# First-norm rows stored four tiles at a time behind phase one, with w2 and the first w3 loads behind the tile transposes

## The chip, the cores and the metric

One NeuronCore of a Trainium2 chip. The metric is device time in microseconds of one execution of the whole kernel, the median of several runs. The engines are named as in the profile: TensorE (PE, with its weight loads as PEld), VectorE (DVE), ScalarE (ACT), GpSimd (POOL) and SyncE (SP), which here only issues DMAs. Sixteen DMA engines move the data for all of them.

## What is computed

The input x has 2048 rows of 1024. It is normalised row by row, xn = norm(x), and the result is a sum of three terms:

```python
xn = layernorm(x)
out = x + A(xn, mem0, Wq, Wk, Wv, Wo, seg_len) + B(xn, w1, w2, w3, w4)
# B: a shifted MLP
h  = gelu(layernorm(xn) @ w1)                 # 1024 -> 1024
hs = shift_quarters(h) @ w2                   # four column groups moved by -1, +1, -2, +2 rows
x1 = xn + hs
B  = x1 + gelu(layernorm(x1) @ w3) @ w4       # 1024 -> 3584 -> 1024
# A: 64 segments of 32 rows; attention of 32 heads over 8 memory rows + 32 rows,
#    the first 8 output rows of a segment are the memory of the next
```

All inputs are bf16. The change touches B's beginning only; A begins after B and reads xn back from a scratch tensor in DRAM.

## The kernel before, in words

Rows are handled in 16 tiles of 128. There are four parts that matter here.

**Phase one** (lines 219 to 405) makes h transposed, `hTB`, in SBUF. For tile n, `load_x(n)` brings the rows in (a ring of ten buffers). `norm_stats(n)` takes the row statistics on VectorE and two powers on POOL (L272): one for the first norm, one for the norm of the norm, which is a different scale of the same row. From tile 8 on POOL also makes a bias `nm2` (L274). `norm2(n)` writes the twice-normed row tile `xn2` (VectorE for n < 8, L281; ScalarE from 8 on, L283). The tile is then transposed: by TensorE for the first six (`tr`, L305), by a DMA transpose on SP's queue from tile 6 on (L285), into `xn2T`, a ring of three pairs of tiles. `stage1` (L321) multiplies one or two tiles by w1, eight column blocks with eight matmuls each, and ScalarE evicts each block with the gelu (L328) through four PSUM buffers. `norm1(n)` writes the once-normed rows into SBUF, `xn_keep` (L291), four tiles to a buffer, and stores them in DRAM as `xn_scratch` (L292, POOL's queue).

**Phase two** (lines 407 to 433) takes 16 tiles through w2 (L417, two halves of eight matmuls), adds `xn_keep` on VectorE (L418), norms with POOL's and ScalarE's help, transposes the result by a DMA on SP's queue (L430) into `xn3T`, and stores x1 in DRAM from POOL's queue (L431).

**Phase three** (lines 435 to 581) is w3, gelu and w4, in four blocks of four tiles (L546 and L572). During its first block the sums of xn over segments are made from `xn_scratch` (L450), and in its last block `xn_scratch` is read again, transposed, for part A (L567). `xn_keep` lives until the end of phase two.

**Part A** follows: L603 (values), L669 (queries and keys), L684 to L727.

The order of work on TensorE, VectorE, ScalarE, POOL and SP is the order in which the program is written; `between` and `prep` say behind which column block of which stage the norms of later tiles are put. A DMA waits on its issuing queue until the transfer that used its semaphore before is finished. There are eight of these semaphores for the hardware queues, used in turn, so at most eight such transfers are open.

w2 is loaded in four pieces of 512 KB on SP's queue ahead of x7 (L250). w3 comes in eight pieces of 896 KB (`load_w3`): two within phase one, two within phase two, four behind it.

Of the kernel before, what the change touches and what calls it, by code (L numbers as in the profile page):

```python
# [27 lines left out]
NT = S // P  # L28
# [49 lines left out]
def kernel(  # L78
# [16 lines left out]
    nc = tc.nc  # L95
# [7 lines left out]
    w2_v = B_w2.rearrange("(k p) n -> p k n", p=P)  # L103
    w3_v = B_w3.rearrange("(k p) n -> p k n", p=P)
# [7 lines left out]
    xn_v = xn_d.rearrange("(n p) d -> p n d", p=P)  # L112
# [78 lines left out]
    with tc.manual_schedule(engines={mybir.EngineType.PE, mybir.EngineType.SP, mybir.EngineType.Pool}), ExitStack() as actx:  # L191
# [6 lines left out]
        with ExitStack() as bctx:  # L198
            w3ctx = bctx.enter_context(ExitStack())
            w3_pool = w3ctx.enter_context(tc.tile_pool(name="w3", bufs=1, side="right"))  # L200
            w3_sb = w3_pool.tile([P, KT, F], BF16)

            w3_at = [0]

            def load_w3():

                c, k0 = divmod(w3_at[0], 4)
                w3_at[0] += 1
                cs = slice(c * (F // 2), (c + 1) * (F // 2))
                nc.sync.dma_start(w3_sb[:, 2 * k0:2 * k0 + 2, cs], w3_v[:, 2 * k0:2 * k0 + 2, cs])  # L210

            with ExitStack() as hctx:
                psum0 = hctx.enter_context(tc.tile_pool(name="psum0", bufs=4, space=PSUM))
# [2 lines left out]
                w2_sb = keep.tile([P, KT, D], BF16)  # L216
                xn_keep = [wpool.tile([P, 4, D], BF16, tag="w", name=f"xnk{i}") for i in range(3)] + [keep.tile([P, 4, D], BF16, name="xnk3")]

                hctx.enter_context(tc.manual_schedule(engines={mybir.EngineType.DVE, mybir.EngineType.Activation}))
                with ExitStack() as p0:  # L220
# [7 lines left out]
                    def load_x(n):  # L228
                        if n < NT:
                            xts[n] = ring.tile([P, D], BF16, tag="xt", bufs=10, name=f"xt{n}")  # L230
                            if n == 0:
                                nc.scalar.dma_start(xts[n][:, 512:], x_v[:, n, 512:])
                                nc.sync.dma_start(xts[n][:, :512], x_v[:, n, :512])
                            else:
                                (nc.gpsimd if n == 12 else nc.sync).dma_start(xts[n][:], x_v[:, n, :])
# [10 lines left out]
                        q.dma_start(w1_sb[:, 2 * c:2 * c + 2, :], w1_v[:, 2 * c:2 * c + 2, :])  # L246
                    for n in range(3, 7):
                        load_x(n)
                    for i in range(4):
                        nc.sync.dma_start(w2_sb[:, 2 * i:2 * i + 2, :], w2_v[:, 2 * i:2 * i + 2, :])  # L250
                    for n in range(7, 10):
                        load_x(n)

                    stats = {}

# [32 lines left out]
                    def norm1(n):  # L288
                        st, mv, ab, rr, nm2 = stats[n]
                        xn = xn_keep[n // 4][:, n % 4]  # L290
                        nc.vector.tensor_scalar(xn, xts[n][:], mv[:, 0:1], rr[:, 0:1], op0=ALU.subtract, op1=ALU.mult)  # L291
                        nc.gpsimd.dma_start(xn_v[:, n, :], xn)  # L292
                        if n < 3:
                            load_x(n + 10)
                        if n in (12, 15):
                            load_w3()
                        return xn

                    def transposes(xn2, xn2T, jj, half, halves=False):
# [21 lines left out]
                    def stage1(n0, nt, xn2T, between, j0=0):  # L321
                        w = nt * P
                        for co in range(KT):
                            ps = psum.tile([P, 512], F32, tag="mm", bufs=4)
                            for k in range(KT):
                                nc.tensor.matmul(ps[:, :w].rearrange("p (n t) -> p n t", t=P), w1_sb[:, k, co * P:(co + 1) * P],  # L326
                                                 xn2T[:, j0:j0 + nt, k, :], start=(k == 0), stop=(k == KT - 1))
                            nc.scalar.activation(hTB[:, co, 2 + n0 * P:2 + n0 * P + w], ps[:, :w], ACTF.Gelu_apprx_tanh)  # L328
                            for f in between.get(co, ()):
                                f()  # L330
# [20 lines left out]
                    def tr(n, half, halves=False):  # L351
                        transposes(xn2s[n], tiles2[n - n % 2], n % 2, half, halves)
# [15 lines left out]
                    for n in range(1, 6):  # L368
                        if n > 1:
                            norm_stats(n + 1, 0)  # L370
                        norm2_of(n)
                        norm_stats(n + 1, 1 if n > 1 else None)
                        if n > 1:
                            norm1(n - 2)
                        if n == 1:
                            stage1_k(tiles2[0])
                        elif n < 4:
                            stage1(n - 1, 1, tiles2[(n - 1) // 2 * 2], {6 - n: [lambda n=n: tr(n, 0)], 7 - n: [lambda n=n: tr(n, 1)]}, (n - 1) % 2)

                    def ahead(n):  # L380
                        norm_stats(n + 1, 0)
                        norm2_of(n)
                        norm_stats(n + 1, 1)
                        if n == 6:
                            norm1(n - 2)

                    stage1(3, 1, tiles2[2], {0: [lambda: tr(4, 0)], 2: [lambda: tr(4, 1), lambda: ahead(6)], 4: [lambda: tr(5, 0)], 5: [lambda: tr(5, 1), lambda: ahead(7)]}, 1)
                    for n in range(13, NT):
                        load_x(n)

                    def prep(n):
                        norm2_of(n)
                        norm_stats(n + 1)
                        if n == 8:
                            norm1(n - 3)
                        norm1(n - 2)

                    for n0 in range(4, NT, 2):
                        between = {c: [] for c in range(KT)}
                        if n0 + 4 < NT:  # L400
                            between[1 + 2 * (n0 == 4)] += [lambda n0=n0: prep(n0 + 4)]
                            between[4 + 2 * (n0 == 4)] += [lambda n0=n0: prep(n0 + 5)]
                        stage1(n0, 2, tiles2[n0], between)
                    for n in (NT - 2, NT - 1):
                        norm1(n)

                xn3T = [wpool.tile([P, 4, KT, P], BF16, tag="w", name=f"xn3T{tb}") for tb in range(4)]
                with ExitStack() as p2:
                    ring = p2.enter_context(tc.tile_pool(name="p2ring", bufs=4))
                    for n in range(NT):  # L410
                        x1 = ring.tile([P, D], F32, tag="x1")
                        st = ring.tile([P, 2, 6], F32, tag="st")
                        for ch in range(2):
                            ps = psum.tile([P, 512], F32, tag="mm", bufs=4)
                            for k in range(KT):
                                o = 2 + n * P + SH[k]
                                nc.tensor.matmul(ps[:], hTB[:, k, o:o + P], w2_sb[:, k, ch * 512:(ch + 1) * 512], start=(k == 0), stop=(k == KT - 1))  # L417
                            nc.vector.tensor_tensor(x1[:, ch * 512:(ch + 1) * 512], ps[:], xn_keep[n // 4][:, n % 4, ch * 512:(ch + 1) * 512], op=ALU.add)  # L418
                            nc.vector.bn_stats(st[:, ch, :], x1[:, ch * 512:(ch + 1) * 512])
                        mv = ring.tile([P, 2], F32, tag="mv")  # L420
                        nc.vector.bn_aggr(mv[:], st[:])
                        a = ring.tile([P, 1], F32, tag="a")
                        nc.vector.tensor_scalar(a[:], mv[:, 1:2], EPS, None, op0=ALU.add)
                        r3 = ring.tile([P, 1], F32, tag="r3")
                        nc.gpsimd.tensor_tensor(r3[:], a[:], neghalf[:, 0:1], op=ALU.pow)
                        nm3 = ring.tile([P, 1], F32, tag="nm3")
                        nc.gpsimd.tensor_scalar(nm3[:], mv[:, 0:1], r3[:], -1.0, op0=ALU.mult, op1=ALU.mult)
                        xn3 = ring.tile([P, D], BF16, tag="xn3")
                        nc.scalar.activation(xn3[:], x1[:], ACTF.Identity, bias=nm3[:], scale=r3[:])
                        nc.sync.dma_start_transpose(xn3T[n // 4][:, n % 4], xn3[:])  # L430
                        nc.gpsimd.dma_start(R1_v[:, n, :], x1[:])  # L431
                        if n in (3, 7):
                            load_w3()

            with ExitStack() as p3:
# [2 lines left out]
                big = p3.enter_context(tc.tile_pool(name="p3big", bufs=1))  # L438
                ring = p3.enter_context(tc.tile_pool(name="p3ring", bufs=2))
                w4_sb = big.tile([P, FT, D], BF16)  # L440
                for _ in range(4):
                    load_w3()
                vbT = big.tile([P, H, NSEG], BF16)
                xb = big.tile([P, KT, NSEG], BF16)
                gps = []
# [95 lines left out]
                for tb in range(4):  # L541
# [18 lines left out]
                    for j in range(4):  # L560
                        n = tb * 4 + j
# [344 lines left out]
    with tc.If(cond > 0):  # L906
        with ExitStack() as fctx:
# [15 lines left out]
            with tc.For_i(0, NSEG, 1) as i:  # L923
# [6 lines left out]
                for which, src in enumerate((Wq_v, Wk_v, Wv_v)):  # L930
                    w = fw.tile([P, KT, H * DH], BF16, tag="w")
# [98 lines left out]
```

## Time and profile before

| | us |
|---|---|
| median of 4 runs | 1508.92 (1508.79 to 1509.85) |
| the profiled execution | 1508.89 |
| its span in the profile | 1506.7 |
| matmul time on TensorE in it | 1501.4 |
| phase one, first matmul to the first of phase two | 1.5 to 67.6 |
| phase two | 67.6 to 122.9 |
| phase three's first block, w3 then w4 | 122.9 to 219.6 (from 171.2 on w4) |

The DMAs issued in and around phase one, from the trace: SP issues the four w2 loads from 8.54 us on, x7 to x11 from 11.56 to 18.21, the transposes of tiles 6 and 7 at 24.49 and 27.16, x13 to x15 from 28.51 to 30.75, the transposes of tiles 8 and 9 at 31.34 and 33.29, the first two w3 loads at 51.27 and 53.88 and the last transpose of the phase, of tile 15, at 52.60. POOL issues the sixteen stores of 256 KB from 15.66 to 47.12 us; they land 4.6 us after they are issued in the median. The granted TensorE clock is 1.00 throughout.

How to read the lines shown below: the page's first part gives the busy time of each engine and its share of the span. A chain of waits is followed back from the last instruction: each line has its start, its length and what ran. A line of the waits names who waited for whom, the total, how often, and the longest. In a table by stretches the busy times come in the order PE, PEld, DVE, ACT, POOL, each with its number of instructions, then the clock, the share of time that the sixteen DMA engines were busy (overlapping packets can take it over 1) and what they moved in GB/s. "T6" and so on is used for the DMA transpose of tile 6 in phase one.

### The profile page before, as it was taken

To read this page: it belongs to the slowest core of one execution; us is meant where nothing else is said; L and a number is where in the kernel's file an instruction comes from. 1 tells how busy PE (TensorE), PEld (TensorE's weight loads), DVE (VectorE), ACT (ScalarE), POOL (GpSimd) and SP (SyncE) were. 2 spreads that over 40 slices of the span, in tenths; PEclk is the share of its full clock that TensorE was granted. 3 is DMA by queue.
4 is the path that set the end of the run, shared out by engine and by line. 5 is a ranking of instruction groups with operands and counts; after the bars stand their busy time and mean duration, and the time that the engine had idled before them with its cause. 6 is when DMAs were issued, how large, how long until landed. Compare 5 with 4: busy or idle time off the path is not lost.

```text
span 1506.7 us, 24319 instructions
## 1 busy us (share of the span) xinstructions
PE 1501.4 (100%) x9828; PEld 803.5 (53%) x9828; DVE 546.6 (36%) x1148; ACT 502.1 (33%) x1140; POOL 175.5 (12%) x250
## 2 busy tenths in 40 slices
PE   9999999999999999999999999999999999999999
PEld 8744444445454444444456645664665455545555
DVE  8382230100010112212246624651564166516643
ACT  5533203013012011111156614660663166406630
POOL 6231020211211221100000000001000100010001
PEclk9999999999999999999999999999999999999999
DMA  9699752453455777622389956992997298928921
GB/s 305 154 265 325 220 172 95 137 203 111 155 154 145 186 236 254 218 98 84 126 219 254 243 130 172 257 233 77 242 247 204 73 230 222 215 66 207 208 50 51
DMA packets 305426, 272.89 MB, mean 181 GB/s; under 512 B 156022, under 2 KB 272536, under 8 KB 305312
## 3 DMA queue, kind: packets, MB, share of 16 engines
q1 hardware_dynamic: 282656, 188.98, 50.0%
q0 software_dynamic: 21824, 81.08, 15.8%
q8 instruction: 79, 1.29, 0.4%
q10 hardware_dynamic: 832, 1.25, 0.2%
q14 instruction: 35, 0.29, 0.1%
HBM read 190.05 MB, written 45.29 MB: 156 GB/s over the span
## 4 chain that ended last, share of the span: by engine, by line
PE 99%; DMA 1%; ACT 0%; DVE 0%; issue 0%; ACTq 0%
PE ps L669 30%; PE pso L727 15%; PE ps L603 15%; PE ps L572 13%; PE ps L546 13%; PE ps L417 4%; PE ps L326 3%; PE psS L684 2%; PE psO L708 2%; DMA xn2T<-xn 1%; PE ps L498 1%; PE ps L867 1%; PE ps L467 0%; PE gps L481 0%; PE warm L343 0%; PE ps L316 0%
## 5 line engine op out<-in xcount | busy, mean ns | idle before, releaser
L669 PE MATMUL ps<-hTb,wt 128*128 128x396 bf16 (+2 forms) x2528 | 484.8, 342 | 0.0
L669 PEld LDWEIGHTS <-wt 128*128 128x128 bf16 x2528 | 236.8, 98 | 175.4 <-DMA wt<-in_A_Wq_dram 0.2
L603 PE MATMUL ps<-wt,xT 128*128 128x512 bf16 x1024 | 221.2, 379 | 0.0
L727 PE MATMUL pso<-wo_sb,oX 128*128 128x512 bf16 (+1 forms) x992 | 209.9, 372 | 0.0
L546 PE MATMUL ps<-xn3T,w_sb 128*128 128x512 bf16 x896 | 196.2, 379 | 0.0
L572 PE MATMUL ps<-w_sb,h3T 128*128 128x512 bf16 x896 | 195.4, 379 | 0.0
L603 PEld LDWEIGHTS <-xT 128*128 128x128 bf16 x1024 | 100.2, 98 | 120.8
L547 ACT ACTIVATE h3T<-ps 128x512 bf16<-128x512 f32 x112 | 67.0, 598 | 290.6 <-PE ps L546 289.7
L727 PEld LDWEIGHTS <-oX 128*128 128x128 bf16 x992 | 96.4, 98 | 107.6
L671 ACT CAST KT<-ps 128x462 bf16<-128x462 f32 (+2 forms) x160 | 81.8, 511 | 202.6 <-PE ps L669 198.4
L572 PEld LDWEIGHTS <-h3T 128*128 128x128 bf16 x896 | 87.1, 98 | 103.5
L546 PEld LDWEIGHTS <-w_sb 128*128 128x128 bf16 x896 | 86.7, 98 | 102.2
L690 DVE TENSOR_REDUCE sums<-sm 99x4 f32<-99x396 f32 (+2 forms) x176 | 97.6, 554 | 114.8 <-ACT sm L688 114.8
L673 ACT ACTIVATE QT<-ps 128x462 bf16<-128x462 f32 (+2 forms) x160 | 84.0, 525 | 120.5 <-PE ps L669 106.2
L605 ACT CAST Vs<-ps 128x512 bf16<-128x512 f32 x64 | 37.5, 586 | 232.1 <-PE ps L603 232.1
L686 DVE TENSOR_TENSOR sm<-psS,c_mask_reg_sb 99x396 f32<-99x396 f32 x152 | 86.7, 570 | 72.3 <-PE psS L684 72.2
L609 DVE CAST Vs<-ps 128x512 bf16<-128x512 f32 x64 | 44.3, 692 | 171.6 <-PE ps L603 171.6
L688 ACT ACTIVATE sm<-sm 99x396 f32<-99x396 f32 (+2 forms) x176 | 92.8, 527 | 34.7 <-DVE sm L686 28.1
L696 DVE TENSOR_TENSOR Pn<-sm,rs 99x396 bf16<-99x396 f32 (+2 forms) x176 | 98.9, 562 | 6.6 <-DMA PT<-Pn 0.7
L734 POOL DMA_DIRECT2D out_dram<-ot x30 | 16.4, 546 | 698.5 <-DVE ot L733 698.5
L573 DVE TENSOR_TENSOR R<-ps,R 128x512 f32<-128x512 f32 x32 | 22.0, 690 | 181.9 <-PE ps L572 173.0
L733 DVE TENSOR_TENSOR ot<-pso,Rt 128x512 bf16<-128x512 f32 (+1 forms) x33 | 22.2, 675 | 166.5 <-PE pso L727 162.3
(131 smaller groups left out, 1049.6 us busy)
## 6 DMA issues: line engine op xcount, KB each, us to landing
wt<-in_A_Wq_dram SPq DMA_DIRECT2D x76, 512.0 KB
wt<-in_A_Wk_dram SPq DMA_DIRECT2D x76, 512.0 KB
wt<-in_A_Wv_dram POOLq DMA_DIRECT2D x24, 1024.0 KB, 6.4
V_scratch<-Vs SPq DMA_DIRECT2D x32, 512.0 KB
V<-V_scratch SPq DMA_DIRECT2D x40, 384.0 KB
R_scratch<-x POOLq DMA_DIRECT2D x16, 512.0 KB, 4.3
R<-R_scratch SPq DMA_DIRECT2D x16, 512.0 KB
R_scratch<-R POOLq DMA_DIRECT2D x16, 512.0 KB, 3.4
```

Of the source, the lines that this page charges most:

```text
L546: nc.tensor.matmul(ps[:].rearrange("p (n t) -> p n t", t=P), w3_sb[:, k, f * P:(f + 1) * P], xn3T[tb][:, :, k, :], start=(k == 0), stop=(k ...
L547: nc.scalar.activation(h3T[:, f, :], ps[:], ACTF.Gelu_apprx_tanh)
L572: nc.tensor.matmul(ps[:], h3T[:, f, j * P:(j + 1) * P], w4_sb[:, f, ch * 512:(ch + 1) * 512], start=(f == 0), stop=(f == FT - 1))
L603: nc.tensor.matmul(ps[:], xT[:, m4 * 4 + j, k, :], wv[:, k, :], start=(k == 0), stop=(k == KT - 1))
L669: nc.tensor.matmul(ps[:, :nb], w[:, k, hh * P:(hh + 1) * P], B["hT"][:, k, :nb], start=(k == 0), stop=(k == KT - 1))
L671: nc.scalar.copy(dst[:, hh, :], ps[:, :nb])
L673: nc.scalar.mul(dst[:, hh, :], ps[:, :nb], scale)
L686: nc.vector.tensor_tensor(sm[:T, :, :T], S3, t["mask"][:].unsqueeze(1).to_broadcast((T, 4, T)), op=ALU.add)
L688: nc.scalar.activation(e[:T, :, :T], sm[:T, :, :T], ACTF.Exp, scale=LN2)
L690: nc.vector.tensor_reduce(ss, e[:T, :, :T], axis=AX.X, op=ALU.add)
L696: nc.vector.tensor_tensor(Pn[:T, :, :T], e[:T, :, :T], rs[:T, :].unsqueeze(2).to_broadcast((T, 4, T)), op=ALU.mult)
L727: nc.tensor.matmul(self.ps[:, :self.w], self.oX[0][:, h, self.oX[1] + self.gl * P:self.oX[1] + (self.gl + 1) * P], wo_sb[:, h, self.cc], s ...
```

## The change

The stores of the once-normed rows leave `norm1`. Behind the last `norm1` there are four stores of four tiles (1 MB) each, on SP's queue. w2 is loaded in two pieces of 1 MB, issued behind `stage1` of tiles 6 and 7 and of tiles 10 and 11, and so on SP behind the transposes of tiles 11 and 15. x13 to x15 are issued behind `stage1` of tiles 4 and 5, which puts them behind the transposes of tiles 8 and 9, where they were ahead of them. The first two w3 loads are issued behind the four stores, and the last four are two of double size.

The order of instructions on TensorE, VectorE and ScalarE stays as it was. On POOL sixteen DMA issues are gone. On SP there are two rows fewer and the order is the new one.

```diff
-            def load_w3():
+            def load_w3(w=1):
 
                 c, k0 = divmod(w3_at[0], 4)
-                w3_at[0] += 1
+                w3_at[0] += w
                 cs = slice(c * (F // 2), (c + 1) * (F // 2))
-                nc.sync.dma_start(w3_sb[:, 2 * k0:2 * k0 + 2, cs], w3_v[:, 2 * k0:2 * k0 + 2, cs])
+                nc.sync.dma_start(w3_sb[:, 2 * k0:2 * (k0 + w), cs], w3_v[:, 2 * k0:2 * (k0 + w), cs])
...
-                    for i in range(4):
-                        nc.sync.dma_start(w2_sb[:, 2 * i:2 * i + 2, :], w2_v[:, 2 * i:2 * i + 2, :])
                     for n in range(7, 10):
                         load_x(n)
+
+                    def load_w2(i):
+                        nc.sync.dma_start(w2_sb[:, 4 * i:4 * i + 4, :], w2_v[:, 4 * i:4 * i + 4, :])
...
                         nc.vector.tensor_scalar(xn, xts[n][:], mv[:, 0:1], rr[:, 0:1], op0=ALU.subtract, op1=ALU.mult)
-                        nc.gpsimd.dma_start(xn_v[:, n, :], xn)
                         if n < 3:
                             load_x(n + 10)
-                        if n in (12, 15):
-                            load_w3()
                         return xn
...
                     stage1(3, 1, tiles2[2], {0: [lambda: tr(4, 0)], 2: [lambda: tr(4, 1), lambda: ahead(6)], 4: [lambda: tr(5, 0)], 5: [lambda: tr(5, 1), lambda: ahead(7)]}, 1)
-                    for n in range(13, NT):
-                        load_x(n)
-
                     def prep(n):
...
                         stage1(n0, 2, tiles2[n0], between)
+                        if n0 == 4:
+                            for n in range(13, NT):
+                                load_x(n)
+                        elif n0 in (6, 10):
+                            load_w2(n0 // 10)
                     for n in (NT - 2, NT - 1):
                         norm1(n)
+                    for i in range(4):
+                        nc.sync.dma_start(xn_v[:, 4 * i:4 * i + 4, :], xn_keep[i][:])
+                    for i in range(2):
+                        load_w3()
...
-                for _ in range(4):
-                    load_w3()
+                for _ in range(2):
+                    load_w3(2)
```

## The prediction

> **What bounds the kernel now.** I read the page first, then the chain of waits and TensorE's waits over phase one, then busy time by stretches, then the queue of SP. The page says that TensorE is the bound:
>
> ```profile
> span 1506.7 us, 24319 instructions
> PE 1501.4 (100%) x9828; PEld 803.5 (53%) x9828; DVE 546.6 (36%) x1148; ACT 502.1 (33%) x1140; POOL 175.5 (12%) x250
> PE 99%; DMA 1%; ACT 0%; DVE 0%; issue 0%; ACTq 0%
> ```
>
> The reader is to see that only 1506.7 - 1501.4 = 5.3 us are left in which the matmul engine does not work, and that the one other entry on the chain, DMA 1%, is the tile transpose xn2T<-xn of phase one. So I look at that. The chain of waits from 20 to 70 us, in order of time (start, us, what):
>
> ```profile
> 24.49 5.48 DMA xn2T<-xn
> 29.97 0.02 issue
> ...
> 30.08 0.69 ACT xn L283
> ...
> 32.14 1.12 ACT xn L283
> 33.26 0.03 ACT hTB L328
> 33.29 6.09 DMA xn2T<-xn
> 39.38 0.14 issue
> 39.52 28.11 PE ps L326 x256
> ```
>
> Call the transpose of tile n Tn. T6, issued at 24.49, lands at 29.97; ScalarE's norm of tile 8 (L283) has waited for it; T9, issued at 33.29, lands at 39.38; TensorE's stage of tiles 8 and 9 starts at 39.52. From there to the end the chain is TensorE alone. TensorE's waits in that window have one entry (us, times, longest):
>
> ```profile
> PE ps L326 <- DMA xn2T<-xn: 0.7, 1, 0.7
> ```
>
> That is not all. From 39.52 on a stage of two tiles takes 64 matmuls; ScalarE's evictions behind every 8 of them come 0.873 us apart when nothing is late (46.70, 47.57, 48.45 in the timeline), so 6.99 us a stage. The first eviction of the stage of tiles 4 and 5 at 25.51 puts that stage's start at about 24.46. Two stages should end at 24.46 + 13.98 = 38.44, and the third starts at 39.52: **1.08 us are lost**, 0.73 in the wait shown and 0.35 at the border near 31.5 us, where ScalarE, held from 28.5 to 30.08 by T6, evicts three PSUM tiles late (31.22).
>
> The rest of phase one has no hole to fill: 11.93 to 24.43 us is 224 matmuls of 128 columns at 55.8 ns = 12.5 us, and the four stages after 39.52 and all of phase two run at an unchanging rate (55.25 us for 256 matmuls, 215.8 ns). The stretches show the room on the DMA side (engines' busy times, then clock, DMA share, GB/s):
>
> ```profile
> 25.00:30.00 5.00, 5.00 (x48) 4.49 (x46) 4.79 (x14) 1.54 (x4) 2.54 (x4) 1.00 1.19 197
> 35.00:40.00 5.00, 4.27 (x40) 3.62 (x39) 4.86 (x13) 3.20 (x8) 4.31 (x7) 1.00 1.20 246
> 60.00:65.00 5.00, 5.00 (x48) 4.48 (x47) 0.00 (x0) 2.11 (x6) 0.00 (x0) 1.00 0.01 5
> ```
>
> The DMA engines are full while T6 to T9 fly and idle from 60 to 75 us.
>
> **The change part by part**, against the profiled execution's own 1508.89 us (span 1506.7 and 2.2 around it; the median is 1508.92, so the two are the same).
>
> *Two w2 loads of 1 MB instead of four of 512 KB ahead of x7.* By 25 us the engines have moved 8.45 MB (the rates of five stretches times 5 us: 196, 386, 376, 381, 352 GB/s), and w2 is 2.1 of it. Without w2 the loads are done some 5.5 us sooner (2.1 MB at 380), so T6 finds empty queues. The x rows come earlier, which gains nothing: VectorE takes them in its own order and is busy 4.79 to 4.92 us of each 5 from 15 to 45 us.
>
> *Sixteen stores of 256 KB leave POOL's queue.* POOL loses 16 issues (10.1 us in all, 0.61 each). It is not on the chain, worth 0. But two of these stores are issued while T6 and T7 fly and five while T8 and T9 do.
>
> *What T6 to T9 then take.* T6 and T9 took 5.48 and 6.09 us. The nearest row with less beside it is the last transpose of phase two: issued 127.20, landed 130.88, so 3.68 us, still beside one 512 KB store. Bounds: 3.7 and 6.1; I take 4. T6 is issued when VectorE has made tile 6 (24.43), which does not move: it lands at 28.5. ScalarE's norm of tile 8 then waits for POOL's nm (29.20 + 0.27 = 29.47) and starts at 29.55 instead of 30.08; T8 at 30.85, tile 9's norm behind its evictions at 31.5, T9 at 32.8, landed at 36.8. TensorE wants it at 38.44; it may take 5.6 us before it costs anything. Both losses go: **-1.08 us**. What is late next is nothing on the path: TensorE itself.
>
> *x13 to x15 pass from before T8 to behind T9* on SP's queue, issued at about 34.1 to 36. VectorE wants x13 at 37.22; it lands at 37 to 38, so VectorE may stop for up to 1 us. Who waits: nm of tile 13 (40.1 + 0.27 before), used by ScalarE only behind the fifth eviction of the stage of tiles 8 and 9, about 43.3. Slack 2.9 us: 0. Behind these loads on SP are T10 and T11: T10 issued at 36, T11 at 37.6 (ScalarE's norm of tile 11 ends at 37.5), wanted when the stage of tiles 10 and 11 starts, 24.46 + 3 x 6.99 = 45.4. With before's 6.1 us and the 0.79 MB of x ahead (2.6 us at 300 GB/s) T11 is there at 46.3 at worst, at 42 to 43 by my 4 us with some of it: cost 0 to 0.9, taken as 0.
>
> *w2's first half behind T11 (about 39), its second behind T15 (about 53).* T12 and T13 stand behind the first half; T13, issued at 44.6, is wanted at 52.4; a megabyte at 300 is 3.5 us: 0. The second half is issued when T15 is (52.60 + 1.23, less 1.0) and lands by 53 + 3.5 + 3 = 59.5 at the slow rate. Phase two's first matmul, which now waits for w2, is at 67.6 - 1.1 = 66.5: cover 7 us, cost 0. Uncovered it would cost its lateness one for one.
>
> *Four stores of 1 MB and two w3 loads (0.92 MB each) behind w2 on SP.* They wait for VectorE's last first norm (45.2, long done) and for SP's older transfers. Phase two's transposes stand behind them. From 53 us the queue holds 1.05 + 4.19 + 1.84 = 7.08 MB; at 386 GB/s (the stretch 150 to 155) 18 us, at 300 (the stretch 55 to 60, transposes and stores mixed) 24 us: empty at 71 to 77. The first transpose of phase two is issued at 75.42 - 1.1 = 74.3. [...]
>
> *Waits.* The built programs say on what the openers of phase two wait: VectorE's first addition and POOL's first power wait for T10 to T15, and not for the stores or w3. Three of SP's transposes of phase two get a wait for a store and two for a w3 load; those stand from 71 to 77 us, the transposes come at 78 to 95.
>
> *Last w3 loads, two of 1.8 MB for four of 0.9.* Same bytes; SP issues two fewer (0.58 us each). They were issued at 128.56 to 131.1 and the second half of w3 is wanted at 122.88 + 14 x 1.727 = 147.1: 3.67 MB at about 400 GB/s (the stretches 135 to 145) end near 140. Cover 6 us: 0.
>
> Sum: 1508.89 - 1.08 = 1507.81, and with a little left at the borders **1507.9**.
>
> **Rivals.**
>
> *The wait only moves* (0.12): T9 is slow because transposes are slow, not because of stores and w2. For it: the share is 1.19 at only 197 GB/s while they fly, so the transposes themselves fill the engines. Against it: 3.68 us for the one at 127.20, at a share of 1.17. If T9 still takes 6.1 from 32.8 it lands at 38.9, and the wait is 0.5: with 0.2 more at the border 1508.3 to 1508.9.
>
> *The queue of SP makes a new wait* (0.12): x13 to x15 ahead of T10 and T11, and w2's megabyte right behind, which shares the engines if they do not finish in order. For it: the share above 1 in every stretch from 25 to 40 us. Against it: no store flies there any more. It decides when T11 lands after 45.4: 37.6 + 6.1 + 2.6 + up to 3.5 = 49.8 would cost up to 4.4 us; half of w2 in its way 2.6. Less the 1.08 gained, 1510.4 (1509.3 to 1512.2): slower than before.
>
> *The stores' queue is slower than any rate here* (in the tail): at 150 GB/s it is empty at 100 us, and the last w3 half comes after 147; +2 to 5 us.
>
> **How the numbers follow.** A measurement of this kernel can tell 0.2%, 3 us, from no change. The likeliest case (0.73) lies between 1507.4 and 1508.4. Faster by 3 us is nearly excluded, since all of TensorE's idle time is 5.3 us, of which 1.5 lie ahead of the first matmul and 3.0 behind the last: 0.02. Slower by 3 us needs the far end of the second rival or something unseen: 0.06. Within: 0.92. The range, 1507.3 to 1509.6, holds the first case and the first rival and leaves out most of the second.
>
> **What would show it.** Right: no wait of TensorE for xn2T; T6 and T9 at about 4 us; the stage of tiles 8 and 9 starting at 38.4 to 38.6 and phase two at 66.5; DMA busy from 60 to 75 us; phase two still 55.2 us. Wrong: a wait for xn2T at the stage of tiles 10 or 12; a wait of TensorE for w2 near 66 or for w3 near 146; T6 still at 5.5 us though the stores are gone.

## The result and the profile after

The changed kernel takes 1508.02 us, the median of 40 runs (1507.26 to 1510.01); the kernel before, run beside it on the same chips, takes 1509.48 (60 runs, 1508.15 to 1511.38). The ratio is 0.9991, with a 95% interval from 0.9986 to 0.9995: about 1.4 us gained (0.75 to 2.1), within the 0.2% that was called no change, and on the gain's side of it. The prediction was 1507.9 in 1507.3 to 1509.6. The execution that was profiled took 1508.82, 0.8 more than its own median, so its span is not the place to look for the gain; phase one is.

The page of the changed kernel, the same three rows as before:

```profile
span 1507.1 us, 24290 instructions
PE 1501.4 (100%) x9828; PEld 803.3 (53%) x9828; DVE 547.0 (36%) x1148; ACT 502.1 (33%) x1140; POOL 167.0 (11%) x234
PE 99%; DMA 1%; SPq 0%; DVE 0%; issue 0%
```

TensorE's busy time is the same to 0.1 us, and POOL has lost its 16 issues (250 to 234). The chain of waits, from 20 us on (start, us, what):

```profile
...
23.90 0.22 PE ps L303 x4
24.12 42.81 PE ps L324 x400
66.94 5.18 PE ps L421 x24
```

Where before had two transposes, a norm and late evictions, there is one piece of 400 matmuls without a hole. TensorE's waits in phase one:

```profile
PE warm L341 <- DVE wz L335: 1.5, 1, 1.5
PE ps L314 <- DMA w_sb<-in_B_w_dram: 0.6, 1, 0.6
```

There is no wait for xn2T. T9, issued at 33.16, landed at 36.30: 3.1 us, where it took 6.09. (The views print no landing for a transpose on SP's queue. The trace has its completion marks, sixteen to a transfer; the landings of transposes given here are the last of these, and for the kernel before they agree with the 29.97 and 39.38 of its chain.) The 0.6 is for a piece of w1 at the very start (before 12.5 us) and has nothing to do with the change; it shifts the whole of phase one. So I measure from the end of TensorE's last own transposes (23.70 before, 24.12 after) to the start of phase two (67.62 and 66.94): 43.92 us before, 42.82 after. **1.10 us are gone; the prediction had 1.08.** This one length serves for every kernel below, and is called "the stretch". It is read from one execution of each, and TensorE does not enter it in step with the transposes (at 23.70 before, with T9 issued at 33.29; at 24.38 in kernel 5, with T9 issued at 33.13): the earlier the entry, the more the same late transpose costs. The DMA side, in slices (busy times, clock, DMA share, GB/s):

```profile
25.00:30.00 5.00, 5.00 (x49) 4.47 (x47) 4.79 (x14) 1.85 (x6) 1.83 (x4) 1.00 0.96 108
35.00:40.00 5.00, 5.00 (x48) 4.48 (x46) 4.66 (x12) 3.53 (x9) 2.79 (x5) 1.00 1.03 256
60.00:65.00 5.00, 5.00 (x48) 4.49 (x46) 0.00 (x0) 2.29 (x6) 0.00 (x0) 1.00 1.05 407
```

While T6 and T7 fly the engines move 108 GB/s where it was 197, and the slice at 60 us, idle before at 5 GB/s, now moves 407: the stores. TensorE is busy 5.00 of 5.00 us in each.

### The profile page after: what moved, and what is told of

Read it like the earlier page. It is cut to its first block, busy times and chain, and to the rows that moved or that the text cites. A ratio compares the mean times of both kernels' runs of the same rounds, so it can differ in the third digit from the quotient of the medians.

```text
span 1507.1 us, 24290 instructions
## 1 busy us (share of the span) xinstructions
PE 1501.4 (100%) x9828; PEld 803.3 (53%) x9828; DVE 547.0 (36%) x1148; ACT 502.1 (33%) x1140; POOL 167.0 (11%) x234
## 3 DMA queue, kind: packets, MB, share of 16 engines
HBM read 190.05 MB, written 45.29 MB: 156 GB/s over the span
## 4 chain that ended last, share of the span: by engine, by line
PE 99%; DMA 1%; SPq 0%; DVE 0%; issue 0%
PE ps L673 30%; PE pso L731 15%; PE ps L607 15%; PE ps L576 13%; PE ps L550 13%; PE ps L421 4%; PE ps L324 3%; PE psO L712 2%; PE psS L688 2%; PE ps L871 1%; PE ps L502 1%; PE gps L485 0%; PE ps L471 0%; DMA w_sb<-in_B_w_dram 0%; DMA wt<-in_A_Wq_dram 0%; PE ps L314 0%
## 5 line engine op out<-in xcount | busy, mean ns | idle before, releaser
L609 ACT CAST Vs<-ps 128x512 bf16<-128x512 f32 x64 | 37.4, 585 | 232.2 <-PE ps L607 232.2
```

## The experiments

Two questions were put to the chip: which part of the change gives the gain, and by what. The theories, by the letters that the expectations use: **S**, the stores beside the transposes made T6 and T9 slow; **W**, the 2.1 MB of w2 in front of them did; then, within S, **B**, it is the bytes of the stores, on whichever queue they wait; **Q**, it is that they wait on another queue than the transposes; and last **P**, it is something of POOL's queue alone. Each kernel is timed beside runs of the kernel before.

### 1. The stores alone

The kernel before, with the stores and the two w3 loads where the change puts them; w2 and x13 to x15 stay at their old places.

```diff
-                        nc.gpsimd.dma_start(xn_v[:, n, :], xn)
-                        if n in (12, 15):
-                            load_w3()
...
+                    for i in range(4):
+                        nc.sync.dma_start(xn_v[:, 4 * i:4 * i + 4, :], xn_keep[i][:])
+                    for i in range(2):
+                        load_w3()
```

> The kernel before with the sixteen stores taken out of phase one and made as four at its end on SP, the first two w3 loads behind them; w2 and x13 to x15 where they were. Theory S (the stores beside T6 to T9 make these slow): the 1.08 us lost between the stage of tiles 4 and 5 and the stage of tiles 8 and 9 fall to 0.2 or less, T8 and T9 take about 3 us; 0.9 us faster than before. Rival W (the two megabytes of w2 ahead of T6 do it): T6 still takes 5 us or more, at least 0.35 us stay lost; 0.0 to 0.7 us faster. Rival M (the wait only moves): a new wait of TensorE for a later transpose, time as before.

Measured: 1508.29 us (13 runs), ratio 0.9991 (0.9982 to 0.9999). Its chain:

```profile
23.82 42.81 PE ps L323 x400
66.64 5.39 PE ps L418 x25
```

The stretch is 42.82 us, as in the changed kernel, with all of w2 still in front of T6. T9, issued at 32.95, landed at 36.04, so 3.1 us, as in the changed kernel. The stores are the whole gain and w2's move adds nothing to it: S stands for T9 and W falls. (T6 took 5.5 us here, which I had put down as W's sign; but in the changed kernel, with w2 away, it took 5.3.)

### 2. w2 alone

The kernel before, with w2 in two late halves and the stores still tile by tile on POOL.

```diff
-                    for i in range(4):
-                        nc.sync.dma_start(w2_sb[:, 2 * i:2 * i + 2, :], w2_v[:, 2 * i:2 * i + 2, :])
...
+                    def load_w2(i):
+                        nc.sync.dma_start(w2_sb[:, 4 * i:4 * i + 4, :], w2_v[:, 4 * i:4 * i + 4, :])
...
+                        if n0 in (6, 10):
+                            load_w2(n0 // 10)
```

> The kernel before with w2 in two halves behind T11 and T15 and nothing else moved; the sixteen stores stay in phase one. Theory S: T9 still flies beside five stores and takes 5 us or more; at least 0.3 of the 1.08 us stay lost. Rival W: T6 takes 3 us, no loss left, 1.1 us faster than before. Either: w2 costs no wait at phase two.

Measured: 1515.5 us (5 runs, 1512.68 to 1517.92), ratio 1.0045 (1.0031 to 1.0059), some 6 us slower than before. Neither theory had that. The chain shows the place:

```profile
31.31 6.64 DMA xn2T<-xn
...
45.78 11.18 DMA xn2T<-xn
...
57.09 14.18 PE ps L327 x128
71.27 0.86 PE ps L420 x4
```

The first row is T8, issued at 31.31, which takes 6.64 us (6.0 before); T9, issued at 33.25, takes 6.3, and TensorE still loses 1.1 us near 38.5. T13, issued at 45.78 behind w2's first half and behind T12 (43.16 to 56.11), takes 11.18 us while POOL's last four stores (44.87 to 47.09) and w2's megabyte are on the way, and TensorE waits 3.3 us for it. So the change's two parts are not independent: w2's new place, which I costed at nothing, is only free because the stores have left.

### 3. The place of x13 to x15

The changed kernel with these loads ahead of T8 again.

```diff
+                    for n in range(13, NT):
+                        load_x(n)
...
-                        if n0 == 4:
-                            for n in range(13, NT):
-                                load_x(n)
-                        elif n0 in (6, 10):
+                        if n0 in (6, 10):
```

> The changed kernel with x13 to x15 back ahead of T8. If the place of these loads matters (rival X: they stood in T8's way), T8 and T9 come later by up to 2 us and some of the 1.08 us is lost again, 0.2 to 0.7. By my theory T9 has 2 us and more to spare: no wait of TensorE, the same as the changed kernel within 0.2 us, and VectorE does not wait 0.2 us for x13.

Measured: 1508.06 us (21 runs), ratio 0.9991 (0.9984 to 0.9997); the stretch, 23.87 to 66.85, is 42.98. Their place does not matter.

### 4. The same late stores on POOL's queue

The changed kernel, one word different: the four stores of 1 MB are issued by POOL.

```diff
-                        nc.sync.dma_start(xn_v[:, 4 * i:4 * i + 4, :], xn_keep[i][:])
+                        nc.gpsimd.dma_start(xn_v[:, 4 * i:4 * i + 4, :], xn_keep[i][:])
```

> The changed kernel with the four stores of 1 MB at the same place but issued by POOL. By my theory when the stores go decides and not which queue they are on: no wait of TensorE in phase one, the same as the changed kernel within 0.3 us. If the queue mattered (stores on SP holding up the transposes of phase two, or POOL's issues holding up its powers), this one differs by 0.5 us or more from the changed kernel.

Measured: 1512.81 us (11 runs), ratio 1.0023 (1.0014 to 1.0032): 4.8 us slower than the changed kernel. (The execution profiled took 1511.81, 1.0 below that median.) I had expected no difference. The stores go out from POOL at 45.29 to 48.38, SP issues T15 at 51.48, and the chain reads:

```profile
51.48 11.09 DMA xn2T<-xn
...
62.71 7.15 PE ps L324 x64
```

TensorE waits 3.2 us for T15. But T15 stands behind T14, issued at 48.86, and T14 landed only at 61.69, T15 at 62.57. So look at what the DMA queues moved from T14's issue on (queue, packets, MB, share), first from 48.9 to 53 us and then from 53.5 to 59:

```profile
DMA packets 370, 1.43 MB, mean 350 GB/s; under 512 B 20, under 2 KB 20, under 8 KB 370
...
q0 software_dynamic: 370, 1.43, 100.9%
```
```profile
q0 software_dynamic: 462, 1.82, 93.3%
q1 hardware_dynamic: 456, 0.12, 9.4%
```

q0 is POOL's queue, q1 SP's. For four microseconds SP's queue moves nothing at all; what keeps T14 out there is not shown. Then it is served, but in 5.5 us T14 gets 0.12 MB through, beside 1.82 MB of stores. What a whole transpose needs can be seen in the changed kernel, in a window (48.5 to 53 us) in which only T14 moves:

```profile
DMA  0000000000000000018999999999910000000000
...
DMA packets 1056, 0.26 MB, mean 58 GB/s; under 512 B 1056, under 2 KB 1056, under 8 KB 1056
```

1056 packets of about 256 B, done in 12 or 13 of the 40 slices of 0.11 us, so 1.4 us; from issue (49.30) to landing (52.33) T14 took 3.0 there. The stores' packets are 1.82 MB / 462 = 3.9 KB.

### 5. The old stores on SP's queue

So I took the kernel before and moved only its 16 stores of 256 KB to SP, at their old times in phase one.

```diff
-                        nc.gpsimd.dma_start(xn_v[:, n, :], xn)
+                        nc.sync.dma_start(xn_v[:, n, :], xn)
```

> The kernel before with its sixteen stores at their old times, 256 KB each, but issued on SP's queue and not on POOL's; w2 and w3 stay. Theory Q (what slows a transpose on SP is data on the other queue, POOL's): with all data on one queue T9 has only what stands ahead of it, takes 3 to 4.5 us, the 1.08 us are gone or down to 0.3; 0.8 to 1.1 us faster than before. Theory B (it is the bytes beside the transposes, on whichever queue): 1 us stays lost, time as before. If SP's waits for VectorE's first norms hold up T6 to T9, it is slower than before by up to 1 us.

Measured: 1508.41 us (13 runs), ratio 0.9992 (0.9984 to 1.0001). The times alone leave it open by a hair; the chain does not:

```profile
24.15 0.22 PE ps L305 x4
24.38 42.95 PE ps L326 x400
67.33 4.75 PE ps L417 x22
```

No wait for xn2T and a stretch of 42.95 us, with the same bytes, at the same places in the program, in the same pieces. The missing wait alone does not decide it: TensorE came 0.68 us later into this stretch than before (24.38 for 23.70) and asked for T9 at about 39.2, so that a T9 of 6.09 us, issued at 33.13, would have cost it some 0.2 us. T9's own time says more: it landed at 38.08, in 4.95 us, 1.1 less than beside POOL's stores, and ahead of it on its own queue stood two stores, which landed at 35.64 and 36.42. That speaks for Q and against B, though 4.95 lies above the 3 to 4.5 that I had given Q.

### 6. w2's second half behind the stores

The changed kernel with `load_w2(1)` behind the four stores on SP, to see what w2's cover of 7 us is worth.

```diff
-                        elif n0 in (6, 10):
-                            load_w2(n0 // 10)
+                        elif n0 == 6:
+                            load_w2(0)
...
+                    load_w2(1)
```

> The changed kernel with the second half of w2 behind the four stores on SP and not ahead of them. It measures the cover of w2: 5.2 MB then stand between T15 (54.5 us) and phase two's need at 66.9 us; at the 390 GB/s of the changed kernel's stretches from 60 to 70 us they are there at 69, so TensorE should wait about 2.4 us at its first matmul with the second half of w2, and the time be 1508.0 + 2.4. If it waits under 0.5 us, w2 had far more cover than I thought; if the prediction's slow rate of 300 GB/s holds, it waits 5 us.

Measured: 1513.26 us (9 runs, 1510.1 to 1514.3), ratio 1.0018 (1.0008 to 1.0028). TensorE's wait, and a stretch behind it (with the granted clock third from the end):

```profile
PE ps L422 <- DMA w_sb<-in_B_w_dram: 3.7, 1, 3.7
```
```profile
67.00:130.00 63.00, 59.29 (x268) 26.47 (x267) 49.27 (x96) 19.20 (x16) 21.33 (x47) 0.97 0.93 255
```

The wait is 3.7 us, where I had expected 2.4 at 390 GB/s; DMA moved 326 GB/s between 60 and 67 us. And it is not all: the 252 matmuls after it take 56.24 us, at 215.8 ns they would take 54.4, so 1.9 us more go with the clock, whose mean in the row above is 0.97. In kernel 4 a wait of 3.2 us, and in kernel 2 one of 3.3, left the clock at 1.00 (kernel 2's in the rows from 55 to 60 and from 67 to 130 us). Kernel 9 below waits 3.5 us, and the row that starts behind its wait shows the loss, beside kernel 4's:

```profile
60.00:67.00 7.00, 4.29 (x40) 3.89 (x41) 0.00 (x0) 1.54 (x4) 0.00 (x0) 1.00 1.07 322
```
```profile
64.00:73.00 9.00, 8.95 (x65) 7.24 (x67) 0.00 (x0) 2.78 (x8) 0.00 (x0) 0.81 0.78 301
```

Of these four waits the two of 3.2 and 3.3 us were not followed by a lower clock, and the two of 3.5 and 3.7 us were. A wait of 3.7 us for w2 cost 1.9 us on top of itself; I had written one for one.

### 7. The stores on POOL in phase two

The changed kernel with the four stores on POOL, behind the first store of phase two.

```diff
-                    for i in range(4):
-                        nc.sync.dma_start(xn_v[:, 4 * i:4 * i + 4, :], xn_keep[i][:])
...
                         nc.gpsimd.dma_start(R1_v[:, n, :], x1[:])
+                        if n == 0:
+                            for i in range(4):
+                                nc.gpsimd.dma_start(xn_v[:, 4 * i:4 * i + 4, :], xn_keep[i][:])
```

> The changed kernel with the four stores of 1 MB on POOL's queue, behind its first store of phase two (about 75 us), so that no transpose of phase one flies beside them. Theory Q: phase one is clean, 66.9 us, without the 3.2 us of the run with POOL's stores at the end of phase one; in phase two SP's first transposes are issued over 2 us or more in place of 1.3, and x1's stores stand behind 4 MB on POOL's queue, so VectorE waits for an x1 buffer about 5 us and TensorE for up to 3; 1508 to 1511. If POOL's issuing of them was the fault (its sequencer, not the data), phase two is not touched and the time is that of the changed kernel.

Measured: 1521.7 us (8 runs, 1511.7 to 1528.51), ratio 1.0074 (1.0051 to 1.0097). That is far outside the 1508 to 1511 that I expected. Phase one is clean (a stretch of 42.81), and then the transposes of phase two fall behind. TensorE's, ScalarE's and VectorE's waits:

```profile
PE ps L551 <- ACT h3T L552: 10.8, 2, 9.5
PE ps L419 <- DVE x L420: 2.8, 3, 1.6
```
```profile
ACT xn L431 <- DMA xn3T<-xn: 37.4, 9, 6.7
```
```profile
DVE x L420 <- DMA R_scratch<-x: 8.2, 3, 5.8
```

ScalarE waits 37.4 us for transposes to free its source buffers. Part of the loss is another thing, though: the R stores of phase two stand on POOL's queue behind the four large ones, and VectorE waits 8.2 us for their buffers. So this kernel agrees with Q but does not price it.

### 8. w1 ahead of x

The changed kernel with the two pieces of w1 that SP issues ahead of x1 and x2, to take the 0.6 us at the start.

```diff
+                        q.dma_start(w1_sb[:, 2 * c:2 * c + 2, :], w1_v[:, 2 * c:2 * c + 2, :])
                         if q is nc.sync:
                             load_x(1 + c // 2)
-                        q.dma_start(w1_sb[:, 2 * c:2 * c + 2, :], w1_v[:, 2 * c:2 * c + 2, :])
```

> The changed kernel with the second and fourth pieces of w1 each one place ahead of x1 and x2 on SP. TensorE waited 0.2 to 0.6 us for the second piece of w1 near 9 us in these runs. If that wait goes and x1, coming 0.7 us later, is still in time, 0.2 to 0.6 us faster than the changed kernel; if x1 is late, the transposes of tile 1 by TensorE wait for it, 0 to 1 us slower.

Measured: 1508.41 us (13 runs), ratio 0.9992 (0.9984 to 1.0001): nothing gained, where I had hoped for 0.2 to 0.6. The wait for w1 stays at 0.6 and waits of 0.8 for the norms join it. Its profiled execution was one that took 1514.8, and shows a way in which this kernel can lose time in single executions:

```profile
PE ps L550 <- DMA w_sb<-in_B_w_dram: 3.5, 1, 3.5
```

The last half of w3 was issued at 136.51, behind SP's transposes, and not near 128 as in the changed kernel's profile. After this wait the clock is down again: its mean from 130 to 230 us is 0.98, where the changed kernel has 1.00, and the 108 matmuls from 151.07 us on take 25.17 us, where 215.8 ns each would make 23.3. The cover of 6 us that the prediction gave w3 is real in most executions and can be used up in one. Why the transposes were late there I have not found.

### 9. The late stores on ScalarE's queue

Kernel 4 left open whether POOL's queue is special. The changed kernel, with the four stores issued by ScalarE behind its norm of tile 14.

```diff
-                        norm1(n - 2)
+                        if n < 15:
+                            norm1(n - 2)
+
+                    def store():
+                        for n in range(13, 16):
+                            norm1(n)
+                        for i in range(4):
+                            nc.scalar.dma_start(xn_v[:, 4 * i:4 * i + 4, :], xn_keep[i][:])
...
+                            if n0 == 10:
+                                between[1] += [store]
```

> The changed kernel with its four stores of 1 MB issued from ScalarE, behind its norm of tile 14, and so on ScalarE's queue (the last first norms stand one hook earlier for it, in the same order on VectorE). Any other queue (Q): large stores on any queue but SP's starve a transpose on SP, so T15, issued near 53.7 us, lands 8 to 11 us later, TensorE waits 2 to 5 us at the stage of tiles 14 and 15, 1510 to 1513.5. POOL's queue alone (P): what starves the transposes is special to the stores issued from POOL; on ScalarE's queue T15 lands in 3 to 5 us, there is no wait for xn2T, and the time is the changed kernel's, 1507.5 to 1509. ScalarE's four issues (about 2.4 us near 49 us) delay evictions that have four PSUM buffers of cover, 3.5 us: 0.

Measured: 1514.12 us (7 runs), ratio 1.0034 (1.0023 to 1.0046). The chain has T15 again, and the queues between 55 and 60 us (q10 is ScalarE's):

```profile
53.29 10.71 DMA xn2T<-xn
```
```profile
q10 hardware_dynamic: 689, 1.38, 91.1%
q1 hardware_dynamic: 687, 0.18, 15.7%
```

P falls: ScalarE's queue does the same as POOL's, and TensorE waits 3.5 us. The two rows show what went through beside what: **689 packets of the stores and 687 of the transposes.** The two queues moved nearly equal numbers of packets (kernel 4: 462 and 456 in 5.5 us), and a packet of the one has 2.0 KB, of the other 256 B. The 687 are T14's: issued at 48.94, it too moves nothing until 53.3, beside 775 packets of stores, and lands at 62.99, T15 behind it at 64.00. (A further 0.8 us of TensorE went to evictions that ScalarE's issues held up; they took 3.4 us in all, and I had set four PSUM buffers against them and written 0. And behind the wait of 3.5 us the 64 matmuls of the last stage took 8.83 us, not 6.99: 1.8 us of lower clock. That is why the time lies above the 1513.5 I had allowed.)

### 10. Smaller stores on POOL's queue

Kernel 4 with sixteen stores of 256 KB for four of 1 MB.

```diff
-                    for i in range(4):
-                        nc.sync.dma_start(xn_v[:, 4 * i:4 * i + 4, :], xn_keep[i][:])
+                    for n in range(NT):
+                        nc.gpsimd.dma_start(xn_v[:, n, :], xn_keep[n // 4][:, n % 4])
```

> The changed kernel with sixteen stores of 256 KB issued from POOL, where the stores on POOL had been four of 1 MB; same place, same bytes, behind the last first norm. If it is the size of the stores that starves T15 (a megabyte is in the way and a quarter of one is not), T15 lands in 3 to 5 us, no wait for xn2T, 1507.5 to 1509. If it is the bytes waiting on POOL's queue, whatever their cut: sixteen issues take about 10 us (0.6 each), 45 to 55, so that the queue fills more slowly and about half of it is done when T15 is issued at 51.5; T15 lands in 6 to 11 us and TensorE waits 0 to 4 us, 1508.5 to 1513.

Measured: 1515.97 us (4 runs), ratio 1.0046 (1.0029 to 1.0062), worse than with large ones and above the 1513 that I had allowed. The chain and TensorE's wait:

```profile
51.55 13.94 DMA xn2T<-xn
```
```profile
PE ps L324 <- DMA xn2T<-xn: 6.0, 1, 6.0
```

POOL issues until 57.1, so stores keep coming while T15 flies. Behind the wait of 6.0 us, again, the last stage took 8.70 us for 6.99, with matmuls of up to 421 ns, where the longest of the same line in the changed kernel takes 273. The cut into pieces is no help: from 53 to 58 us POOL's queue moved 454 packets and 1.53 MB, SP's 489 packets and 0.12 MB.

The stretches side by side (from the end of TensorE's own transposes to phase two):

| kernel | stores | from, to (us) | stretch (us) |
|---|---|---|---|
| before | POOL, 16, within phase one | 23.70, 67.62 | 43.92 |
| changed | SP, 4, at its end | 24.12, 66.94 | 42.82 |
| 1 | SP, 4, at its end, w2 early | 23.82, 66.64 | 42.82 |
| 5 | SP, 16, within phase one | 24.38, 67.33 | 42.95 |
| 2 | POOL, 16, within phase one, w2 late | 23.70, 71.27 | 47.57 |
| 4 | POOL, 4, at its end | 23.51, 69.85 | 46.34 |
| 9 | ScalarE, 4, near its end | 23.76, 72.87 | 49.11 |
| 10 | POOL, 16, at its end | 23.76, 74.33 | 50.57 |

In this table the stretch is 42.8 to 43.0 us with the stores on SP's queue and 43.9 to 50.6 with them on another. In kernels 9 and 10, 1.8 and 1.7 us of this are the longer last stage behind the wait.

## Why the prediction was right, and where its reasons were not

**The size: right; the place: right for the larger part.** The 1.08 us that were to go are the 1.10 us that went. By the starts of TensorE's matmuls before, 0.89 of it was lost at 38.5 us, waiting for T9, and 0.22 near 31.4, behind the late evictions (my 0.73 and 0.35 divide about the same sum otherwise). The 0.89 went for the reason given: T9 took 3.1 us, below my 4, so that term was mis-sized on the safe side. What is late next is TensorE itself, as written: the kernels without a wait (changed, 1, 3, 5) lie within 0.4 us of one another.

**T6 at 4 us, from 28.5 on: wrong, and the gain of the 0.2 us behind it luck.** T6 landed at 29.80 in the changed kernel, 5.3 us after its issue at 24.48, with neither stores nor w2 beside it; before it took 5.48. My own sign of being wrong, "T6 still at 5.5 us though the stores are gone", all but came true. Kernels 1 and 3 show it too, with T6 issued at 24.14 and 24.41 and ScalarE's norm of tile 8 waiting for it:

```profile
29.74 1.24 ACT L283 ACTIVATE xn<-xt,nm,rr 128x1024 bf16<-128x1024 bf16 x1 [1.11 <-DMA xn2T<-xn]
```
```profile
30.20 1.24 ACT L284 ACTIVATE xn<-xt,nm,rr 128x1024 bf16<-128x1024 bf16 x1 [1.52 <-DMA xn2T<-xn]
```

In the changed kernel this norm starts at 29.96, 0.16 us behind T6's landing (the view names VectorE's factors, but those are tile 9's), and not at 29.55. What the late evictions then cost TensorE goes with how far into the stretch T6 lands: at 6.27 us before and 6.17 in kernels 3 and 4, 0.2 us are lost each time; at 5.68 in the changed kernel and 5.82 in kernel 1, nothing. The changed kernel had TensorE 0.42 us later than before, by its wait for w1, and that has nothing to do with the change. Why T6, the first transpose by DMA, takes 5 us in every kernel stays open: between 27 and 28 us only 42 packets move, before and after alike.

**"Two w2 loads instead of four ahead of x7 ... so T6 finds empty queues": wrong as a cause.** Kernel 1 keeps w2 in front and has the same stretch, and in the changed kernel, with empty queues, T6 was as slow as ever. Of the two causes that I named together only one acted, on T9, and the prediction had no way to tell which.

**"By my theory when the stores go decides and not which queue they are on" (expected of kernel 4): wrong, the step that failed.** I took the gain from the stores being gone from beside T6 and T9, and gave the queue that they move to no part in it. T14, alone in the changed kernel, had its 1056 packets of about 256 B through in 1.4 us. In kernel 4, beside the stores on POOL's queue, it had 456 through in 5.5 us, next to 462 of theirs; in kernel 9, beside ScalarE's, 687 in 5 us, next to 689. Nor is that all, since for the 4 us before it had none. With the stores on the transposes' own queue, issued behind T15, TensorE does not wait: T14 took 3.0 us to land and T15 4.9 (51.92 to 56.86), for 12.8 and 11.1 in kernel 4. So the queue is, as far as these runs show, part of what makes the change gain, and the one word in kernel 4 is worth 4.8 us at the end of phase one. What makes two queues share in this way is not shown. That word sets two things together: the queue, and when the stores leave (45.29 to 48.38 on POOL; from 53.83, behind T15, on SP). The forecast held because the change put the stores on SP; with the same reasons I would have forecast the same for kernel 4 (1507.9 for 1512.81).

Such counts are shown for the transposes at the end of phase one in kernels 4 and 9. For T9 of the kernel before they are not: stores of POOL move beside it, and taking them away (kernel 1) or to SP's queue (kernel 5) shortens it, by 3.0 and 1.1 us.

**x13 to x15, up to 1 us of VectorE: right.** It waits 0.20 us, which reaches nobody:

```profile
37.48 0.69 DVE L266 BATCH_NORM_STATS2 st<-xt 128x6 f32<-128x512 bf16 x1 [0.20 <-DMA xt<-in_A_x_dram]
```

**w2 late, cost 0: right, but only with the stores gone** (kernel 2: 6 us). Its price when uncovered was above one for one (kernel 6: 1.9 us on top of a wait of 3.7).

**The stores' 7.08 MB on SP, empty at 71 to 77 us: right.** DMA moves 376 to 407 GB/s from 60 to 75 us, the first transpose of phase two is issued at 74.73, and phase two takes 55.25 us, as before. That phase two's transposes lose nothing behind these bytes was an estimate, with no run to show it. In the changed kernel the transfers of SP's queue landed here in the order of their issue: the stores at 63.68 to 71.91, w3 at 74.20 and 76.46, the transpose at 78.67, 3.9 us after its issue (3.1 before), and TensorE reads its tile from 122 us on.

**The rivals.** The wait did not stay, and no new one came at the stage of tiles 10 and 12. The one on the slow side (SP's queue holds T11 up) was aimed at the wrong place: TensorE waited for a transpose of phase one only in the kernels before, 2, 4, 9 and 10, each with bytes on another queue beside it.

## What to carry to other kernels

In this kernel the bulk stores belong on the queue whose small-packet transfers must not be late, behind them, and not on a free engine's queue: here one word (which engine issues four stores) is worth 4.8 us, and cutting the stores smaller makes it worse (1515.97 us for 1512.81). When two causes are named for one slow transfer, try each alone before the second is moved; the move of w2, harmless in the change, costs 6 us by itself. Before a wait is costed one for one, look at the granted clock behind it: here it stayed at 1.00 behind waits of 3.2 and 3.3 us and was lower behind waits of 3.5 and 3.7.

## What the runs showed of the hardware that was not expected

- Two busy queues moved nearly equal numbers of packets, 689 and 687 in 5 us in kernel 9 (2.0 KB and 256 B) and 462 and 456 in 5.5 us in kernel 4 (3.9 KB and 256 B); the transpose in kernel 9 then had 0.18 of 1.57 MB. Done alone its packets take 1.4 us; T15 took 10.7 to 13.9 us to land in kernels 4, 9 and 10, in 4 and 9 behind a T14 that had waited with it. Ahead of this T14 moved nothing for 4 us in both, which equal counts do not explain.
- The first transpose by DMA took 5.0 to 5.6 us to land in the kernels before, changed, 1, 3 and 5, whatever moved beside it; a later one alone took 3.0.
- The issue of a transpose can be held up as well: in kernel 4 T15 kept SP for 7.86 us, where the median of its kind in the changed kernel is 1.23. In kernel 10 the longest was 2.99 and the landing later still (13.94 us after issue, for 11.09), so the late landing came without the long issue too.
- Waits of TensorE of 3.2 and 3.3 us (kernels 4 and 2) cost nothing more, with the granted clock at 1.00 behind them. Waits of 3.5, 3.7 and 6.0 us (kernels 9, 6 and 10) cost another 1.8, 1.9 and 1.7 us: about the same in each case. The granted clock behind them was 0.81 from 64 to 73 us in kernel 9, and from 67 to 130 us 0.97 in kernel 6 and 0.99 in kernel 10.
